# Chunk attention into a squared-ReLU FFN on one core: order of the input loads, casts behind a copy, and the first slice of w_in issued by ScalarE

## The chip, the cores and the metric

The kernel runs on one core of one Trainium2 chip. The time is the device time of one execution in microseconds (us). TensorE (PE), VectorE (DVE), ScalarE (ACT), GpSimd (POOL) and SyncE (SP) each run their own instructions in order and wait for each other by semaphores. DMAs are started by an instruction on one of these engines and are carried by 16 DMA engines.

## The reference

```python
def _attn_ref(q, k, v):                      # q, k, v: 8 x 8 x 576 x 64, float32
    # chunks of 64 tokens attend to themselves alone
    scores = scale * np.matmul(q_c, k_c.transpose(0, 1, 2, 4, 3))
    attn = np.exp(scores - np.max(scores, axis=-1, keepdims=True))
    attn = attn / (np.sum(attn, axis=-1, keepdims=True) + 1e-09)
    return np.matmul(attn, v_c)
...
x = attn_out.transpose(0, 2, 1, 3).reshape(B * S, H * D)      # 4608 x 512
h = np.maximum(x @ w_in, 0.0)                                 # w_in: 512 x 2048
return (h * h @ w_out).astype(np.float32)                     # w_out: 2048 x 512
```

## The kernel before, in words

The 4608 tokens are 18 groups of 256 tokens (four chunks of 64), and two groups are a block of 512 tokens: nine blocks, j = 0 to 8. Each block goes through the FFN in bfloat16: `ffn_in` or, from block 2 on, `ffn_in_unit` (x @ w_in, ReLU, square; the matmuls are at L607 and L494), and then `ffn_out` (L664; block 0 has its own `ffn_out_by_ft`, L781). Blocks 1 to 8 use a Strassen-like scheme with sums and differences of quarters, whose parts are named n, m, n1, n2.

Attention for later groups is put between the FFN's matmuls. The FFN of a block is a generator, and each of its steps is a slot. A table (`plan`) written by hand says after which slot a piece of attention comes, and on which slots (`go_slots`) one DMA load of a later group is issued. Pieces have short names: C casts q and k of a group to bfloat16 (CQ and CK each alone, L334 and L341; on GpSimd for groups under 8, then on ScalarE), TD transposes them by one DMA (L352, tile qkT), SC is the scores (L375) and exp (L386), AV the product with V (L403) with its division (L410, L411), XT the transpose of x (on PE, L430, with a copy at L435, for groups under 6; by DMA, L424, tile xT, from group 6 on). `nxt` is the block after the current one and `far` the one after that.

All loads and all DMA transposes are issued by SyncE, in the order in which the program says them, so that a load that stands ahead of a transpose in the program also goes ahead of it in the queue. Each DMA waits for the one eight places before it to have landed. Loads of q and k are `qk_pieces` (L106, L117, L120), those of V `v_pieces` (L148, L152): five for an even group (two of even heads, three of odd heads), four for an odd one.

The opening works on block 0 by halves of its heads: four loads of q and k (L228), eight of V (L237, into the space of `w_sum`), then the eight slices of w_in (L163), each 512 KB of float32, cast by GpSimd into `w_in_bf` (L166; the first in two halves), and the slices of w_out (L171, cast at L174). Float32 slices share five buffers named `w_st`. While PE transposes, scores and weights the first 512 tokens, `keep_busy` (L327) puts matmuls without use between. The first FFN matmul (L607) needs the first slice of w_in.

Of the kernel before, what the change touches and what calls it, by code (L numbers as in the profile page):

```python
# [17 lines left out]
def kernel(  # L18
# [9 lines left out]
    nc = tc.nc  # L28
# [128 lines left out]
        for f in pieces:  # L157
            f()

    def load_w_in(i, n_cast=1):  # L160
        cols = slice(i * 256, (i + 1) * 256)
        st = wst_pool.tile([128, 1024], FP32, name="w_st").rearrange("p (a f) -> p a f", a=n_dt)
        nc.sync.dma_start(out=st, in_=moe_w_in[:, cols].rearrange("(a p) f -> p a f", p=128))  # L163
        n = 256 // n_cast
        for c in range(0, 256, n):
            nc.gpsimd.tensor_copy(  # L166
                out=w_in_bf[:, :, i * 256 + c:i * 256 + c + n], in_=st[:, :, c:c + n])
# [77 lines left out]
    def transpose_half(src, dst, copies, by_token=False):  # L245
        flat = dst.rearrange("c t h q -> c (t h q)")
        n = 1024 // len(copies)
        if len(copies) == 1:
            banks = [bank_bf16()] * 2
            at0 = (0, 512)  # L250
        else:
            banks = [bank_bf16(), bank_bf16()]
            at0 = (0, 0)
        for h in range(2):
            cols = banks[h][:, at0[h]:at0[h] + 512].rearrange("c (n i p) -> c i n p", n=8, i=4)
            for i in range(4):
                for a in range(2):
                    nc.tensor.transpose(
                        out=cols[64 * a:64 * a + 64, i],
                        in_=src[:, 2 * h + a, i, 1::2],  # L260
                        identity=ident)
        for i, copy in enumerate(copies):
            out_, in_ = flat[:, i * n:(i + 1) * n], banks[i][:, 0:n]
            if by_token:
                out_ = out_.rearrange("c (n p i) -> c n p i", n=8, i=4)
                in_ = in_.rearrange("c (n i p) -> c n p i", n=8, i=4)
            copy(out=out_, in_=in_)
# [23 lines left out]
    def values_half(e, x, u, j):  # L291
        v_bf = v_first.bitcast(BF16)
        ps = ps_att.tile([128, 2, 512], FP32, name="ps_att")
        for t in range(2):
            for h in range(2):
                for a in range(2):
                    for p in range(2):
                        o0 = (2 * t + h) * (D + 1)
                        nc.tensor.matmul(
                            out=ps[64 * p:64 * p + 64, a, o0:o0 + D + 1],  # L300
                            lhsT=e[64 * p:64 * p + 64, a, h, 2 * j + t, :],
                            rhs=v_bf[64 * p:64 * p + 64, 2 * j + t, 4 * u + 2 * h + a, 1::2],
                            start=True, stop=True)
        o = ps[:, :, 0:4 * (D + 1)].rearrange("p a (h d) -> p a h d", d=D + 1)
        rec = att_pool.tile([128, 2, n_hp], FP32, name="rec", bufs=4)
        nc.vector.reciprocal(out=rec, in_=o[:, :, :, D])
        nc.vector.tensor_tensor(
            out=x[:, 4 * j:4 * j + 4].rearrange("p b a d -> p a b d"),
            in0=o[:, :, :, 0:D],
            in1=rec.to_broadcast([128, 2, n_hp, D]),  # L310
            op=ALU.mult)
# [494 lines left out]
    def pieces(grps):  # L806
        for g in grps:
            yield from qk_pieces(g)
        for g in grps:
            yield from v_pieces(g)  # L810
# [7 lines left out]
        kh.append(load_half(k, u, "k_sb"))  # L818
    for u in range(2):
        load_v_half(u)  # L820
    load_w_in(0, n_cast=2)
    xTs[0] = att_pool.tile([128, BT // 128, n_dt, 128], BF16, name="xT", bufs=2)
    qkTs = [att_pool.tile([128, 2, 2, n_hp, 128], BF16, name="qkT", bufs=4) for _ in range(2)]
    xs = [att_pool.tile([128, 2, n_hp, 2, D], BF16, name="x", bufs=3).rearrange(
# [8 lines left out]
    transpose_half(qh[1], qkTs[1][:, 0], [V])  # L833
    keep_busy(2)
    transpose_half(kh[1], qkTs[1][:, 1], [V, A], by_token=True)
    values_half(e0, xs[0], 0, 0)
    keep_busy(2)
    e1 = scores_half(qkTs[1])
# [34 lines left out]
    for j, grps in enumerate(blocks):  # L873
        nxt = blocks[j + 1] if j + 1 < len(blocks) else []
        far = blocks[j + 2] if j + 2 < len(blocks) else []
        plan = {}

        def at(slot, f, g):
            plan.setdefault(slot, []).append((f, g))

        if j == 0:
            loads, go_slots = pieces(far), range(17)
            at(28, sum_quarters(b11_p_b21, b11, b21), None)
            for slot, f in ((24, TA), (27, SC), (29, AV), (31, XT)):
                at(slot, f, nxt[0])
            at(31, TQ, nxt[1])
            at(31, TK, nxt[1])
            at(31, sum_quarters(b11_m_b22, b11, b22, ALU.subtract), None)
            phases = [first_ffn_in, ffn_out_by_ft(0)]
        elif j == 1:  # L890
            loads, go_slots = itertools.chain(*map(qk_pieces, far)), range(26, 48)
            for slot, f in ((4, SC), (8, AV), (12, XT)):
                at(slot, f, grps[1])
            for i, g in enumerate(nxt):
                for slot, f in ((16 + 4 * i, C), (21 + 4 * i, TD), (36 + i, SC), (38 + 2 * i, AV),
                                (41 + 2 * i, XT)):
                    at(slot, f, g)
            for i, g in enumerate(far):
                at(36 + 4 * i, C, g)
                at(42 + 3 * i, TD, g)  # L900
            at(2, sum_quarters(b11_p_b12, b11, b12), None)
            at(12, sum_quarters(b12_p_b22, b12, b22), None)
            at(20, sum_quarters(b21_p_b22, b21, b22), None)
            phases = [ffn_in(1, [(0, 256, FT_ORDER), (256, 256, FT_ORDER)]), ffn_out(1)]
        else:
            loads, go_slots = pieces(far), range(32)
            slots = {SC: (4, 4), AV: (7, 11), XT: (10, 14), C: (18, 22), TD: (20, 24)}
            if j == 3:
                slots.update({SC: (8, 8), AV: (10, 14), XT: (13, 17)})
                go_slots = [*range(6), *range(13, 17), *range(20, 32)]  # L910
            if not is_whole(nxt[0] if nxt else 0):
                slots.update({SC: (6, 8), AV: (10, 14), XT: (12, 16)})
            if j == 2:
                loads = itertools.chain(*map(v_pieces, nxt), loads)
                slots = {SC: (8, 10), AV: (12, 15), XT: (15, 18), C: (20, 23), TD: (22, 25)}
                go_slots = [*range(16), *range(25, 36)]
            late_by = 0
            if j in UNITS:
                late_by = 3
            if j == 2:  # L920
                slots.update({AV: (12, 16), XT: (15, 19)})
                go_slots = [*range(16), *range(28, 39)]
            elif j in UNITS:
                go_slots = range(35)
                if far and is_whole(far[0]):
                    go_slots = [*range(6), *range(13, 17), *range(23, 35)]
                slots.update({SC: (4, 4), AV: (8, 13), XT: (12, 17)})
                if j == 3 or not is_whole(nxt[0] if nxt else 0):
                    slots.update({SC: (8, 8), AV: (11, 16), XT: (14, 19)})
            for f in (SC, AV, XT):  # L930
                for i, g in enumerate(nxt):
                    at(slots[f][i], f, g)
            if j > 2 and far and is_whole(far[0]):
                for slot, f, i in ((16, CQ, 0), (18, CK, 0), (18, TD, 0), (18, CQ, 1),
                                   (19, CK, 1), (19, TD, 1)):
                    at(slot + late_by, f, far[i])
            else:
                for f in (C, TD):
                    for i, g in enumerate(far):
                        at(slots[f][i] + late_by, f, g)  # L940
            phases = [ffn_in_unit(j) if j in UNITS else ffn_in(j, [(0, BT, FT_ORDER)]),
                      ffn_out(j)]
        slot = 0
        for phase in phases:
            for _ in phase:
                if slot in go_slots:
                    for f in loads:
                        f()
                        break
                for f, g in plan.get(slot, []):  # L950
                    f(g)
                while late and (slot >= LATE_STORES.get(j, 99) or (j, slot) == (2, 9)):
                    late.pop(0)()
                slot += 1
        assert all(x < slot for x in plan), (j, slot, sorted(plan))
        go(loads)
        while late and j > 1:
            late.pop(0)()
# [30 lines left out]
```

## Time and profile before

| | |
|---|---|
| median of 3 runs | 280.36 us (279.69 to 280.68) |
| the profiled execution | 282.07 us, span 280.3 us |
| PE busy | 269.5 us (96%) |
| mean granted clock of TensorE | 0.993 |
| DMA queue of SyncE | 54.67 MB, 84.8% of 16 engines' span |

In the profile a line names an engine, a line of the kernel, an operation and its tiles, out<-in. Matmul records overlap, and a few can be missing. "Idle before" is time in which the engine had nothing running, with what ended it. The landing time of a DMA is when its semaphore was raised; it is read from the trace beside the issue. The clock is that which was granted to TensorE, 1.00 being full speed. Times are from the start of the span.

### The profile page before, as it was taken

To read this page: it belongs to the slowest core of one execution; us is meant where nothing else is said; L and a number is where in the kernel's file an instruction comes from. 1 tells how busy PE (TensorE), PEld (TensorE's weight loads), DVE (VectorE), ACT (ScalarE), POOL (GpSimd) and SP (SyncE) were. 2 spreads that over 40 slices of the span, in tenths; PEclk is the share of its full clock that TensorE was granted. 3 is DMA by queue.
4 is the path that set the end of the run, shared out by engine and by line. 5 is a ranking of instruction groups with operands and counts; after the bars stand their busy time and mean duration, and the time that the engine had idled before them with its cause. 6 is when DMAs were issued, how large, how long until landed. Compare 5 with 4: busy or idle time off the path is not lost.

```text
span 280.3 us, 7376 instructions
## 1 busy us (share of the span) xinstructions
PE 269.5 (96%) x3047; PEld 186.2 (66%) x3047; DVE 205.2 (73%) x313; ACT 155.7 (56%) x262; POOL 95.4 (34%) x110
## 2 busy tenths in 40 slices
PE   6987999999999999899999999999999999999995
PEld 4642445788785678457855785578558855885684
DVE  0542704899888798689868795979589949786794
ACT  1544713787426765579265927583779185507710
POOL 2036868351043810172017301720190019003403
PEclk9997999999999999999999999999999999999999
DMA  6999999989999879999999999897699992204004
GB/s 230 234 337 336 303 347 243 310 223 214 181 223 170 208 234 205 246 272 235 204 212 267 219 186 294 190 153 165 152 295 224 180 274 39 40 22 130 0 0 152
DMA packets 141313, 57.11 MB, mean 204 GB/s; under 512 B 110368, under 2 KB 135200, under 8 KB 141280
## 3 DMA queue, kind: packets, MB, share of 16 engines
q1 hardware_dynamic: 140544, 54.67, 84.8%
q0 software_dynamic: 592, 1.84, 1.7%
q8 instruction: 24, 0.39, 0.6%
q10 hardware_dynamic: 144, 0.13, 0.1%
q14 instruction: 9, 0.07, 0.1%
HBM read 36.70 MB, written 9.44 MB: 165 GB/s over the span
## 4 chain that ended last, share of the span: by engine, by line
PE 50%; DVE 0%; issue 0%
PE ps_ffn L664 24%; PE ps_ffn L607 19%; PE ps_ffn L494 6%; PE ps_att L403 1%; PE ps_att L375 1%; DVE o_sb L769 0%
## 5 line engine op out<-in xcount | busy, mean ns | idle before, releaser
L607 PE MATMUL ps_ffn<-xT,w_in_bf 128*128 128x512 bf16 (+1 forms) x528 | 112.7, 357 | 2.9 <-POOL w_in_bf L166 2.0
L620 POOL TENSOR_TENSOR gT<-rl 128x512 bf16<-128x512 f32 x40 | 45.5, 1152 | 121.5 <-ACT rl L571 118.3
L607 PEld LDWEIGHTS <-w_in_bf 128*128 128x128 bf16 x528 | 50.9, 99 | 40.8 <-POOL w_in_bf L166 2.5
L664 PEld LDWEIGHTS <-w_st 128*128 128x128 bf16 x640 | 62.2, 98 | 7.7 <-issue 0.4
L571 ACT ACTIVATE rl<-ps_ffn 128x512 f32<-128x512 f32 x84 | 50.0, 596 | 30.4 <-PE ps_ffn L607 30.2
L620 DVE TENSOR_TENSOR w_st<-gT 128x2048 bf16<-128x2048 bf16 x40 | 47.4, 1219 | 6.0 <-ACT gT L574 5.9
L664 PE MATMUL ps_ffn<-w_out_bf,w_st 128*128 128x256 bf16 x384 | 45.1, 273 | 0.0
L620 DVE TENSOR_TENSOR gT<-rl 128x512 bf16<-128x512 f32 x30 | 20.7, 691 | 21.1 <-ACT rl L571 20.7
L664 PE MATMUL ps_ffn<-w_sum,w_st 128*128 128x256 bf16 x256 | 29.6, 273 | 0.2 <-ACT n L737 0.2
L664 PEld LDWEIGHTS <-gT 128*128 128x128 bf16 x256 | 24.7, 98 | 5.0 <-ACT gT L574 0.5
L602 DVE TENSOR_TENSOR gT<-rl 128x256 bf16<-128x256 bf16 (+1 forms) x41 | 18.5, 491 | 10.2 <-ACT rl L598 9.8
L598 ACT ACTIVATE rl<-ps_ffn 128x256 bf16<-128x256 f32 (+1 forms) x48 | 20.3, 455 | 9.6 <-PE ps_ffn L607 8.9
L511 DVE SCALAR_TENSOR_TENSOR gT<-rl 128x512 bf16<-128x512 f32 x21 | 23.2, 1103 | 0.4
L411 DVE TENSOR_TENSOR x<-ps_att,rec 128x512 bf16<-128x512 f32 x32 | 22.1, 691 | 1.1
L771 ACT COPY o_sb<-ps_ffn 128x512 f32<-128x512 f32 x7 | 4.1, 585 | 30.4 <-PE ps_ffn L664 30.4
L386 ACT ACTIVATE e<-ps_att 128x1024 bf16<-128x1024 f32 x16 | 15.8, 1023 | 5.4 <-PE ps_att L375 5.4
L494 PEld LDWEIGHTS <-w_dif 128*128 128x128 bf16 x140 | 13.1, 98 | 7.5
L664 PE MATMUL ps_ffn<-w_out_bf,gT 128*128 128x256 bf16 x128 | 15.6, 273 | 0.0
L664 PE MATMUL ps_ffn<-w_sum,gT 128*128 128x256 bf16 x128 | 15.3, 273 | 0.0
L166 POOL CAST w_in_bf<-w_st 128x1024 bf16<-128x1024 f32 (+1 forms) x9 | 8.7, 969 | 19.0 <-DMA w_st<-in_moe_w_in_dram 19.0
L620 DVE TENSOR_TENSOR w_st<-xT 128x1024 bf16<-128x1024 bf16 (+1 forms) x21 | 12.5, 652 | 2.8 <-DMA xT<-x 2.0
L781 PE MATMUL ps_ffn<-w_out_bf,gT 128*128 128x512 bf16 x64 | 14.5, 380 | 0.0
(82 smaller groups left out, 294.2 us busy)
## 6 DMA issues: line engine op xcount, KB each, us to landing
q_sb<-in_q_dram SPq DMA_DIRECT2D x16, 512.0 KB, 6.4
k_sb<-in_k_dram SPq DMA_DIRECT2D x24, 256.0 KB, 6.0
out_dram<-o_sb SPq DMA_DIRECT2D x12, 512.0 KB, 4.3
w_st<-in_moe_w_in_dram SPq DMA_DIRECT2D x8, 512.0 KB, 8.6
w_st<-in_moe_w_out_dram SPq DMA_DIRECT2D x8, 512.0 KB, 6.0
ve_sb<-in_v_dram SPq DMA_DIRECT2D x28, 128.0 KB, 3.2
vo_sb<-in_v_dram SPq DMA_DIRECT2D x21, 128.0 KB, 3.1
k_sb<-in_k_dram SPq DMA_DIRECT2D x4, 512.0 KB, 6.8
```

Source lines behind the costliest of these rows:

```text
L166: nc.gpsimd.tensor_copy(out=w_in_bf[:, :, i * 256 + c:i * 256 + c + n], in_=st[:, :, c:c + n])
L386: nc.scalar.activation(out=e_out, in_=s_in, func=AF.Exp, scale=scale)
L411: nc.vector.tensor_tensor(out=x[:, t].rearrange("p h a d -> p a h d"), in0=o[:, :, :, 0:D], in1=rec.to_broadcast([128, 2, n_hp, D]), op=AL ...
L494: nc.tensor.matmul(out=out[:, 256 * f:256 * f + 256], lhsT=a[:, d, 128 * f:128 * f + 128], rhs=b[:, :, d, :], start=(first and f == 0 and ...
L511: later.append(lambda: nc.vector.scalar_tensor_tensor(out=place_of(i, jj), in0=both(x), scalar=0.0, in1=both(x), op0=ALU.max, op1=ALU.mult))
L571: nc.scalar.activation(out=rl, in_=h, func=AF.Relu)
L598: nc.scalar.activation(out=rl[:, 0:n], in_=h[:, 0:n], func=AF.Relu)
L602: nc.vector.tensor_tensor(out=gT[:, ft, c:c + n], in0=rl[:, 0:n], in1=rl[:, 0:n], op=ALU.mult)
L607: nc.tensor.matmul(out=h[:, 0:n], lhsT=w_in_bf[:, dt, ft * 128:(ft + 1) * 128], rhs=xT[:, c // 128:(c + n) // 128, dt, :], start=(dt == 0) ...
L620: engine.tensor_tensor(out=out, in0=in0, in1=in1, op=op)
L664: nc.tensor.matmul(out=outs[t], lhsT=a[:, i, t * 128:(t + 1) * 128], rhs=b[:, i, :], start=(first and i == 0 and (last or t == 0)), stop=( ...
L781: nc.tensor.matmul(out=o_ps[tt], lhsT=gT[:, ft, tt * 128:(tt + 1) * 128], rhs=w_out_bf[:, ft, :], start=(ft == 0), stop=(ft == n_ft - 1))
```

## The change

Five things are moved. No arithmetic changes, and all sizes stay.

- w_in's first slice is issued by ScalarE, behind its copy of the second half of k's transposes and ahead of the second exp, and no longer by SyncE behind V.
- In block 0 the loads are q and k of groups 4 and 5 and V of group 4. V of group 5 becomes the first loads of block 1 (slots 26 on), behind the two DMA transposes of groups 4 and 5 (slots 21 and 25).
- In block 1 XT of group 3 comes after slot 13, not 12.
- In block 2 the loads are issued on slots 0 to 11, 20 to 22 and 28 to 38, not on 0 to 15 and 28 to 38. What went out on slots 12 to 15 (q and two k of group 9, and one V) now comes behind the two XT (slots 15 and 19).
- In block 3 CQ, CK and TD of group 11 come after slots 25, 26 and 26 (with the 3 of `late_by`), not after 21, 22 and 22.

In the order of instructions on the engines, this puts: on SyncE, the transposes of groups 4 and 5 ahead of four V loads; the two xT transposes of block 3's x ahead of q, k, k and one V load; group 11's transpose behind four V loads. On ScalarE, the copy of n2 (L737) of block 3 ahead of both casts of group 11, one ReLU (L598) ahead of the copy of xT (L435) of group 3, and the DMA of w_in's first slice between a copy (L267) and an exp (L286). GpSimd's order is the same.

```diff
-    def load_w_in(i, n_cast=1):
+    def load_w_in(i, n_cast=1, queue=nc.sync):
...
-        nc.sync.dma_start(out=st, in_=moe_w_in[:, cols].rearrange("(a p) f -> p a f", p=128))
+        queue.dma_start(out=st, in_=moe_w_in[:, cols].rearrange("(a p) f -> p a f", p=128))
...
     for u in range(2):
         load_v_half(u)
-    load_w_in(0, n_cast=2)
...
     transpose_half(kh[1], qkTs[1][:, 1], [V, A], by_token=True)
+    load_w_in(0, n_cast=2, queue=nc.scalar)
     values_half(e0, xs[0], 0, 0)
...
         if j == 0:
-            loads, go_slots = pieces(far), range(17)
+            loads = itertools.chain(*map(qk_pieces, far), v_pieces(far[0]))
+            go_slots = range(17)
...
         elif j == 1:
-            loads, go_slots = itertools.chain(*map(qk_pieces, far)), range(26, 48)
-            for slot, f in ((4, SC), (8, AV), (12, XT)):
+            loads = itertools.chain(v_pieces(nxt[1]), *map(qk_pieces, far))
+            go_slots = range(26, 48)
+            for slot, f in ((4, SC), (8, AV), (13, XT)):
...
             if j == 2:
                 slots.update({AV: (12, 16), XT: (15, 19)})
-                go_slots = [*range(16), *range(28, 39)]
+                go_slots = [*range(12), *range(20, 23), *range(28, 39)]
...
             if j > 2 and far and is_whole(far[0]):
-                for slot, f, i in ((16, CQ, 0), (18, CK, 0), (18, TD, 0), (18, CQ, 1),
-                                   (19, CK, 1), (19, TD, 1)):
+                q1, k1 = (22, 23) if j == 3 else (18, 19)
+                for slot, f, i in ((16, CQ, 0), (18, CK, 0), (18, TD, 0), (q1, CQ, 1),
+                                   (k1, CK, 1), (k1, TD, 1)):
```

## The prediction

> **What bounds the kernel now.** I read the busy times first, then the slices, the waits of TensorE, the opening in order of time, and SyncE's queue around each wait.
>
> ```profile
> PE 269.5 (96%) x3047; PEld 186.2 (66%) x3047; DVE 205.2 (73%) x313; ACT 155.7 (56%) x262; POOL 95.4 (34%) x110
> PE   6987999999999999899999999999999999999995
> PEclk9997999999999999999999999999999999999999
> ```
>
> TensorE (PE) is the bound: 280.3 - 269.5 = 10.8 us without a matmul in the whole span. Only where PE waits, or where its clock drops, can an edit of order change the time. Its waits:
>
> ```profile
> PE ps_ffn L607 <- POOL w_in_bf L166: 2.0, 1, 2.0
> ...
> PE ps_ffn L607 <- DMA xT<-x: 0.9, 1, 0.9
> ...
> PE ps_att L375 <- DMA qkT<-qkb: 0.5, 1, 0.5
> PE ps_att L430 <- DVE x L411: 0.4, 1, 0.4
> ...
> PE ps_ffn L664 <- ACT n L737: 0.2, 1, 0.2
> ```
>
> Four of these stand where the change reorders: 0.9 (at 113.10), 0.5 (74.89), 0.4 (59.90), 0.2 (135.87). The fifth, 2.0 at 22.93, is the opening's. The opening in order of time (start, length, engine, line; in brackets idle time before it and what ended it), then busy times by stretch with the granted clock:
>
> ```profile
> 2.89 9.25 SPq L237 DMA_DIRECT2D w_sum<-in_v_dram  x8
> 12.19 11.08 SPq L163 DMA_DIRECT2D w_st<-in_moe_w_in_dram  x8
> 16.26 1.17 POOL L166 CAST w_in_bf<-w_st 128x512 bf16<-128x512 f32 x2 [13.98 <-DMA w_st<-in_moe_w_in_dram]
> 17.66 1.04 POOL L166 CAST w_in_bf<-w_st 128x1024 bf16<-128x1024 f32 x1 [0.24 <-DMA w_st<-in_moe_w_in_dram]
> 21.83 1.04 POOL L166 CAST w_in_bf<-w_st 128x1024 bf16<-128x1024 f32 x1 [3.12 <-DMA w_st<-in_moe_w_in_dram]
> 22.93 7.26 PE L607 MATMUL ps_ffn<-xT,w_in_bf 128*128 128x512 bf16 x25 [2.01 <-POOL w_in_bf L166]
> ```
>
> ```profile
> 20.59:24.00 3.41, 1.40 (x7) 0.51 (x6) 0.43 (x1) 1.32 (x4) 1.81 (x2) 1.00 1.08 363
> 24.00:27.41 3.41, 3.41 (x9) 1.21 (x8) 1.67 (x2) 1.36 (x3) 2.57 (x3) 0.50 0.96 321
> ```
>
> The eight slices of w_in, w0 to w7, land at 16.20, 17.61, 21.77, 23.18, 24.64 and so on: 1.3 to 1.5 apart, but 4.16 between w1 and w2. PE uses up w0 and w1 by 20.92 and waits 2.01 for w2's cast. After that stretch, 41% busy, the granted clock is 0.50 for 3.41 us, which costs half of it, 1.71. So the late w2 costs 3.7 us in this execution.
>
> **The change, part by part.** The profiled execution took 282.07 (span 280.3 and 1.8 around it); the median of the runs is 280.36, which is 1.71 less. That is the price of the clock drop, so I suppose, without proof, that most runs lack the drop. The sum is made against the profiled execution and carried over to the median.
>
> *1. V of group 5 leaves the loads of block 0 and goes behind two DMA transposes of block 1.* SyncE before:
>
> ```profile
> 64.52 1.06 SPq L148 DMA_DIRECT2D ve_sb<-in_v_dram  x2
> 65.62 1.16 SPq L152 DMA_DIRECT2D vo_sb<-in_v_dram  x2
> 66.95 5.60 SPq L352 DMA_TRANSPOSE qkT<-qkb  x2
> ```
>
> The first two rows are V of group 5 (448 KB, landing 67.39 to 68.99). The transposes land at 72.92 and 74.85, and PE's scores start 0.04 after each, the second after 0.51 of idleness. With V out of the way the first can be issued at 64.5, 2.4 earlier, and the second once Pool's k cast ends at 65.29. Both then land before their scores at 72.96 and 74.38: -0.51. V lands behind them at about 73, and values of group 5 first need it at 78.58, so it is hidden there. The queries of groups 6 and 7 follow on the same queue; they had been issued at 73.07, behind the transposes' 5.60, and should go up to 2 us sooner.
>
> *2. In block 2 the loads stop after slot 11, so that three loads of group 9 (q and two k) and one of V no longer stand ahead of the two xT transposes.* Before:
>
> ```profile
> 99.31 3.82 SPq L106 DMA_DIRECT2D q_sb<-in_q_dram  x1
> 103.17 1.78 SPq L120 DMA_DIRECT2D k_sb<-in_k_dram  x2
> 105.00 1.60 SPq L148 DMA_DIRECT2D ve_sb<-in_v_dram  x1
> 106.70 4.27 SPq L424 DMA_TRANSPOSE xT<-x  x2
> ```
>
> VectorE finishes both x by 101.4; xT lands at 112.21 and 113.05, while PE is free at 112.20. Without the 7.2 us of issuing ahead, xT lands near 106: -0.90. What is late next is group 9: its q and k land behind two xT transposes, about 1.8 later (111.2 for the last against 109.39). ScalarE casts them in order, and only its L771 copy at 112.23 stands behind, so it moves by little; the group's transposed q and k have 2.24 us of room (landing 117.73, scores at 119.97). 0.
>
> *3. In block 3 the casts of group 11 go behind the copy of n2 on ScalarE.* Before, and SyncE's transposes after them:
>
> ```profile
> 134.28 1.05 ACT L341 CAST qkb<-k_sb 128x1024 bf16<-128x1024 f32 x1 [0.64 <-DMA k_sb<-in_k_dram]
> 135.24 0.58 ACT L737 COPY n<-ps_ffn 128x512 f32<-128x512 f32 x1
> 136.91 4.60 SPq L352 DMA_TRANSPOSE qkT<-qkb  x2
> ```
>
> PE waited 0.25 for that copy: -0.25. The new cost is on SyncE: group 11's transpose now stands behind four V loads. They took 2.3 us to issue (141.56 to 143.83) and 448 KB to move, landing over 3.85 us after the transpose. Its landing was 143.59 for scores at 145.36, 1.77 of room. With PE 1.66 earlier the room is 0.11; with the transpose 2.3 later, 2.2 us would be missing, unless the queue runs ahead by the 2 us of part 1. The queue shows no pause from 88 to 146, so what it gains at 73 it should keep. Bounds 0 and +3.7 (3.85 later against 0.11 of room); I take +0.3, near the first, since 2.3 less 2 is left.
>
> *4. In block 1 the transposes of x of group 3 go one slot back.* The 0.38 at 59.90 waits for x, ready at 59.84. The ScalarE copy behind it (60.33 to 61.34) must end before PE's unit 16, at 61.42 by three units of 0.43. One slot later, the transposes end at the same time, as x is no earlier; PE does unit 13 first and then lacks it at unit 16. The relu of unit 13 (0.38) also comes ahead of the copy. Bounds -0.38 and +0.4; I take +0.05: the wait moves.
>
> *5. w0 goes to ScalarE's queue.* ScalarE's own issue of an output store lasts 0.37 and SyncE's of a w_in slice 0.37 to 0.51. It stands between the copy that ends at 11.82 and the exp at 12.34, and fits into the 0.52 idle there: 0 to +0.2. What it is moved past is V: pieces 6 to 8 land at 13.54, 14.08 and 14.61, and PE takes them at 13.76 and 15.57, so there is 0.22 and 0.96 of room. w0 is worth 1.4 us of the engines (the spacing of slices), so these can come 0 to 1.4 later and the first FFN matmul (17.30) up to 13.54 + 1.4 - 13.76 = 1.2 later. The 2.01 for w2 behind it covers that. If w2 came in time, the 1.2 would show. w0 itself gains nothing: its cast begins at 16.26 and PE is busy with attention until 17.30. w1 to w7 leave SyncE one place (0.55) sooner, but the bytes ahead of w2 are the same. Bounds for the opening: -3.7 (no wait, no drop) and +1.2; I take -0.2, near no change, as the lateness of w2 is not one of issue.
>
> The row 22.93 puts the cost in arrival, 2.01. The Trainium skill, "DMA: Bandwidth & Descriptors", section "Issuing engines are not separate DMA queues", speaks against the move: transfers share the same 16 engines whoever starts them, and a second issuer saves issue time alone. By it the opening would gain at most w_in's issue time of 0.5; no run here shows it yet.
>
> The clock row gives 0.50 after 41% busy. The skill's page "TensorE: Matmul & The Clock Gate", section "Part 1: The HAM clock gate (the "warmup" mystery)", calls the activity window free-running; by it the same idle time may or may not cost the 1.71.
>
> Sum: -0.51 - 0.90 - 0.25 + 0.3 + 0.05 - 0.2 = -1.5. Profiled: 280.6; median: 280.36 - 1.5 = 278.9.
>
> **The rivals.** *A, group 11 late (slower):* if the queue is not ahead by 145 us, TD of group 11 lands up to 3.85 later against 1.77 of room in the old time; then all earlier gains are swallowed there and the end is +2.1, 282.4. It decides from a delay of 1.77 on, and is measurably slower from 2.6. For it: the landings of those four loads; against: part 1's 2 us. *B, half of that:* the delay is about 1.8 to 2, PE waits off its gain, and the time is 280.4: no change; V late in an opening where w2 is in time (+1.2 against -1.3) gives the same, 280.3. *C, w2 comes in time:* two rings instead of one let it land near 19.0 (17.61 + 1.4); the wait goes too, in place of the -0.2 of part 5: 280.36 - 1.3 - 2.0 = 277.1. Against it: the bytes ahead of w2 are the same.
>
> **How the numbers follow.** Changes below 0.3% (0.84 us) can't be told from none. My case 0.50 (its own range 278.0 to 279.7), C 0.10, B 0.22, A 0.18. The range reaches from C's 277.0 to short of A's end, 281.2, and leaves out half of A's chance and little else. Faster: 0.47 of my case (its range passes 279.5) + 0.10 = 0.57; same: 0.22 + 0.03 = 0.25; slower 0.18.
>
> **What would show it.** Right: TensorE's waits at 74.9, 113.1 and 135.9 are gone; the first xT transpose is issued before 102; a wait for xT by ScalarE's copy near 61; the q10 queue carries w0 and V's last pieces land after 14.6. Wrong: a wait of PE for qkT near 144 over 0.5 us, the exp at 12.34 more than 0.3 later, or w2 landing before 20.

## The result, and the profile after

The changed kernel takes 283.35 us in the median of four runs (282.45 to 284.23), against 280.40 for the kernel before in four runs beside it: a ratio of 1.0109, 95% interval 1.0064 to 1.0154. It is about 3 us slower, where 1.5 us less was forecast, and lies beyond the forecast range (281.2). Run again (e9 below) it gives 1.0100 (1.0056 to 1.0145). Ratios here and below leave out executions over 1.5% above the fastest of their kernel.

The profiled execution of the changed kernel took 282.45 us (span 280.7). That is only 0.4 more than the 282.07 of the profiled execution of the kernel before, though the medians lie 3 apart; "The base of the sum" below takes this up. Its busy times, the slices, and the two queues that issue loads (packets, MB, share of 16 engines' span):

```profile
PE 270.2 (96%) x3044; PEld 187.0 (67%) x3047; DVE 203.2 (72%) x313; ACT 155.9 (56%) x262; POOL 96.0 (34%) x110
...
PE   7879999999999999999979999999999999999995
...
PEclk9979999999999999999979999999999999999999
...
q1 hardware_dynamic: 140016, 54.15, 83.7%
...
q10 hardware_dynamic: 672, 0.66, 0.8%
```

The new mark is the 7 at the twenty-first slice, in PE's row and in the clock's: something near 144 us holds PE up and then halves its clock. The queue q10 now carries w0 (0.66 MB, against 0.13 before). The view of waits of PE (us in total, times, longest) names it:

```profile
PE ps_att L375 <- DMA qkT<-qkb: 2.1, 1, 2.1
PE ps_ffn L327 <- POOL ident L72: 1.7, 1, 1.7
PE ps_att L299 <- DMA w_sum<-in_v_dram: 1.0, 3, 0.5
...
PE ps_ffn L607 <- ACT xT L435: 0.2, 1, 0.2
```

The 2.0 for w2's cast, the 0.9 for xT, the 0.5 for qkT, the 0.4 for x (L430) and the 0.2 for n2's copy are all gone. In their place stand 1.0 for V in the opening and 2.1 for a transposed q and k. The timeline of PE places the latter: group 11's 32 matmuls of scores, behind the 32 of group 10.

```profile
140.70 1.03 PE L607 MATMUL ps_ffn<-xT,w_in_bf 128*128 128x512 bf16 x4
141.66 0.45 PE L375 MATMUL ps_att<-qkT 64*64 64x64 bf16 x32
144.17 0.65 PE L375 MATMUL ps_att<-qkT 64*64 64x64 bf16 x32 [2.07 <-DMA qkT<-qkb]
```

The timeline of SyncE's queue shows what stood ahead of that transpose (start, length of the issue):

```profile
132.50 1.26 SPq L424 DMA_TRANSPOSE xT<-x  x1
133.86 1.91 SPq L352 DMA_TRANSPOSE qkT<-qkb  x1
135.82 0.58 SPq L152 DMA_DIRECT2D vo_sb<-in_v_dram  x1
136.45 1.10 SPq L148 DMA_DIRECT2D ve_sb<-in_v_dram  x2
137.59 0.51 SPq L152 DMA_DIRECT2D vo_sb<-in_v_dram  x1
138.19 2.39 SPq L352 DMA_TRANSPOSE qkT<-qkb  x1
```

Group 10's transpose goes out at 133.86, then four V loads, then group 11's at 138.19. They land at 138.81 (group 10), 139.31 to 140.89 (V) and 144.13 (group 11), and PE goes on 0.04 after that. The casts of group 11 had ended by 133.4, so ScalarE is not the cause. That the place in the queue is, e15 tests below. Busy times by stretch with the granted clock (PE, PEld, DVE, ACT, POOL, clock, DMA share, GB/s):

```profile
137.28:140.70 3.42, 3.42 (x22) 1.91 (x20) 2.18 (x5) 2.02 (x4) 0.00 (x0) 1.00 1.08 195
140.70:144.11 3.41, 1.40 (x38) 0.63 (x35) 0.97 (x2) 2.35 (x4) 1.04 (x1) 1.00 1.03 295
144.11:147.53 3.42, 3.36 (x42) 1.89 (x43) 0.69 (x1) 1.02 (x2) 0.00 (x0) 0.50 1.01 284
```

After a stretch that is 41% busy (1.40 of 3.41) the clock is 0.50 for 3.42 us, as it was in the opening of the kernel before. So in this execution the late transpose costs 2.07 and then about 1.71, half of the 3.41 (an estimate).

The account by blocks, from the first L607 matmul of each block's FFN:

| block | 0 | 1 | 2 | 3 | 4 | 5 | end |
|---|---|---|---|---|---|---|---|
| before | 17.30 | 52.46 | 84.38 | 113.10 | 141.10 | 168.56 | 280.29 |
| after | 18.37 | 51.07 | 82.42 | 110.09 | 137.67 | 168.93 | 280.67 |
| after less before | +1.07 | -1.39 | -1.96 | -3.01 | -3.43 | +0.37 | +0.38 |

Up to block 4 the change had gained 3.43 us. In block 4 it lost 3.80, which is the wait and the clock (2.07 + 1.71 = 3.78).

The opening: ScalarE issued w0 at 10.55, which took 0.43 us beside its copy of 10.54 to 11.12; it then stood idle for 0.99 until the exp at 12.12 (12.34 before), so the issue cost it nothing. V's last two pieces landed at 15.73 and 16.58 (14.08 and 14.61 before), and PE waited for them. From the timeline of the opening:

```profile
10.55 0.43 ACTq L163 DMA_DIRECT2D w_st<-in_moe_w_in_dram  x1
...
15.77 0.32 PE L299 MATMUL ps_att<-w_sum,e 64*64 64x65 bf16 x8 [0.32 <-DMA w_sum<-in_v_dram]
...
16.62 0.32 PE L299 MATMUL ps_att<-w_sum,e 64*64 64x65 bf16 x8 [0.53 <-DMA w_sum<-in_v_dram]
...
18.37 12.81 PE L607 MATMUL ps_ffn<-xT,w_in_bf 128*128 128x512 bf16 x52
...
20.53 1.04 POOL L166 CAST w_in_bf<-w_st 128x1024 bf16<-128x1024 f32 x1 [1.17 <-DMA w_st<-in_moe_w_in_dram]
```

The FFN starts 1.07 later, and w2 (landed 20.47, cast from 20.53) is in time for it. PE runs 52 matmuls without a wait, the first of them at a clock of 0.50 (17.82 to 21.23).

### The profile page after: what moved, and what is told of

It is laid out like the page before. It is cut to its first block, busy times and chain, and to the rows that moved or that the text cites. A ratio compares the mean times of both kernels' runs of the same rounds, so it can differ in the third digit from the quotient of the medians.

```text
span 280.7 us, 7374 instructions
## 1 busy us (share of the span) xinstructions
PE 270.2 (96%) x3044; PEld 187.0 (67%) x3047; DVE 203.2 (72%) x313; ACT 155.9 (56%) x262; POOL 96.0 (34%) x110
## 4 chain that ended last, share of the span: by engine, by line
PE 85%; DMA 5%; SPq 5%; DVE 3%; issue 1%; ACT 0%; DVEq 0%
PE ps_ffn L607 34%; PE ps_ffn L664 32%; PE ps_ffn L494 8%; PE ps_ffn L781 5%; SPq L237 3%; PE ps_att L403 2%; DMA qkT<-qkb 2%; DMA w_sum<-in_v_dram 2%; PE ps_att L375 2%; DMA ve_sb<-in_v_dram 2%; DVE w_st L620 1%; SPq L352 1%; PE ps_att L430 1%; SPq L228 1%; PE ps_att L191 1%
## 5 line engine op out<-in xcount | busy, mean ns | idle before, releaser
L607 PE MATMUL ps_ffn<-xT,w_in_bf 128*128 128x512 bf16 (+1 forms) x528 | 113.3, 359 | 0.2 <-ACT xT L435 0.2
L607 PEld LDWEIGHTS <-w_in_bf 128*128 128x128 bf16 x528 | 51.3, 99 | 38.0 <-issue 2.8
L598 ACT ACTIVATE rl<-ps_ffn 128x256 bf16<-128x256 f32 (+1 forms) x48 | 20.4, 454 | 8.6 <-PE ps_ffn L607 7.8
L602 DVE TENSOR_TENSOR gT<-rl 128x256 bf16<-128x256 bf16 (+1 forms) x41 | 16.9, 456 | 9.2 <-ACT rl L598 8.8
L574 ACT ACTIVATE gT<-rl 128x512 bf16<-128x512 f32 x21 | 13.2, 630 | 0.7
```

The source lines that it names most:

```text
L574: nc.scalar.activation(out=gT[:, ft], in_=rl, func=AF.Square)
L598: nc.scalar.activation(out=rl[:, 0:n], in_=h[:, 0:n], func=AF.Relu)
L602: nc.vector.tensor_tensor(out=gT[:, ft, c:c + n], in0=rl[:, 0:n], in1=rl[:, 0:n], op=ALU.mult)
L607: nc.tensor.matmul(out=h[:, 0:n], lhsT=w_in_bf[:, dt, ft * 128:(ft + 1) * 128], rhs=xT[:, c // 128:(c + n) // 128, dt, :], start=(dt == 0) ...
```

## The experiments

Two theories stood at first. *Queue place* (T in the expectations): group 11's transpose behind four V loads is the whole loss, and the other parts are gains. *Opening* (rival O): w0 on ScalarE's queue makes V late, and what was gained there in one execution is lost in most. From the first runs came two more: that part 2 (block 2) makes the last piece of group 8's V late, so that two late pieces took the gains (D), and that SyncE's queue carries too much in any order (rival F). Every ratio is to the kernel before on the same chip, with its 95% interval.

| run | kernel | ratio |
|---|---|---|
| e1 | after, part 3 undone | 1.0041 (1.0004 to 1.0077) |
| e2 | before, part 3 alone | 1.0102 (1.0054 to 1.0149) |
| e3 | after, part 5 undone | 1.0185 (1.0136 to 1.0235) |
| e4 | before, part 5 alone | 1.0011 (0.9982 to 1.0040) |
| e5 | after, both late pieces earlier | 0.9981 (0.9947 to 1.0016) |
| e6 | after, part 3 undone, V of group 8 earlier | 1.0021 (0.9988 to 1.0053) |
| e7 | before, part 1 alone | 1.0004 (0.9973 to 1.0034) |
| e8 | before, part 2 alone | 1.0031 (0.9996 to 1.0067) |
| e9 | after, again | 1.0100 (1.0056 to 1.0145) |
| e10 | e5 with fewer V loads | 0.9974 (0.9944 to 1.0003) |
| e11 | before with fewer V loads | 0.9971 (0.9939 to 1.0003) |
| e12 | e5, part 5 undone | 1.0028 (0.9994 to 1.0061) |
| e13 | e15, and V of group 8 one slot earlier | 1.0019 (0.9988 to 1.0049) |
| e14 | e13, part 5 undone | 1.0030 (1.0003 to 1.0057) |
| e15 | after, group 11's transpose first | 1.0029 (1.0005 to 1.0054) |

e1 to e4, e5 to e8, e9 to e12 and e13 to e15 each shared a chip.

**Part 3 out, and part 3 alone.** e1 takes it out of the changed kernel, e2 puts it alone into the kernel before:

```diff
-                q1, k1 = (22, 23) if j == 3 else (18, 19)
-                for slot, f, i in ((16, CQ, 0), (18, CK, 0), (18, TD, 0), (q1, CQ, 1),
-                                   (k1, CK, 1), (k1, TD, 1)):
+                for slot, f, i in ((16, CQ, 0), (18, CK, 0), (18, TD, 0), (18, CQ, 1),
+                                   (19, CK, 1), (19, TD, 1)):
```

> The changed kernel with part 3 undone (group 11's casts and transpose back at slots 21 and 22). Theory T (group 11's transpose behind four V loads makes TensorE wait 2.07 at 144 and drops the clock for 3.41, some 1.7): that wait goes, the small one for the copy of n2 (0.25) comes back, and the time falls by 2.0 + 1.7 - 0.25 = 3.5 from 283.35, to about 279.9. Rival O (the slowdown is the opening's, by w0 on ScalarE's queue): at most 1 falls away, 282.4 or more.

> The kernel before with part 3 alone. Theory T: without the head start of the other parts the transpose of group 11 lands some 2.3 to 3.9 later than 143.59, against 1.77 of room: a wait of 0.3 to 2.1 less the 0.25 of the copy, and up to 1.7 of clock where the wait is long: 280.5 to 283.9. Rival O: 280.1 to 280.4, no wait for qkT above 0.5 near 145.

Part 3 alone makes the kernel before 1.0% slower, as much as the whole change does. Without it the changed kernel is 0.4% slower: part 3 is the larger part of the loss. The 279.9 us expected of e1 did not come (281.34, and 279.52 for the kernel before beside it): undoing part 3 gave back about half of the 3.5 us that T reckoned. In e2's waits stands the same line as after:

```profile
PE ps_att L375 <- DMA qkT<-qkb: 2.2, 1, 2.2
```

In e1 it is gone (group 11's transpose lands at 142.91, its scores begin at 144.54), but another has come, which the prediction did not speak of. The timeline of PE in e1:

```profile
119.36 0.19 PE L403 MATMUL ps_att<-vo_sb,e 64*64 64x65 bf16 x1
121.58 0.19 PE L403 MATMUL ps_att<-vo_sb,e 64*64 64x65 bf16 x1 [2.04 <-DMA vo_sb<-in_v_dram]
```

That is the last piece of group 8's V. Part 2 puts it behind a 512 KB store of the output; group 9's transpose stood ahead of it before as well. It landed at 119.56 before, with its matmuls at 122.18; in e1 it landed at 121.54, with PE there at 119.5.

**w0 back on SyncE, and part 5 alone.** e3 undoes part 5 in the changed kernel, e4 makes it alone:

```diff
-    load_w_in(0, n_cast=2, queue=nc.scalar)
...
         load_v_half(u)
+    load_w_in(0, n_cast=2)
```

> The changed kernel with w0 issued by SyncE behind V again. Theory T alone: the wait at 144 stays at about 2 and the time stays within 1 of 283.35; V pieces land evenly, PE waits none for V in the opening. Rival O: the time falls by 1.5 to 3, to 280.4 to 281.9.

> The kernel before with w0 issued by ScalarE, nothing else. Theory T: the opening's delay for V (0.9 of waits in the changed kernel, first FFN matmul 1.07 later) is covered by the wait for the third slice, so 280.4 give or take 0.8. Rival O: 281.4 to 283.4, with V's last pieces at about 16.6 and the first FFN matmul at 18.4.

e4 is no different from the kernel before: the opening theory falls, and with it every gain or loss of over 0.4% by this part alone. In its profile the first FFN matmul is at 17.90 and PE waits 0.94 and 0.92 for slices of w_in. e3 is not better than the changed kernel but looks worse, beyond what either theory expected (285.35 us); its profile has both late pieces, 2.60 for V of group 8 and 2.81 for qkT.

**Both late pieces brought forward.** e5 keeps all five parts, but issues the rest of block 2's loads without the pause of slots 23 to 27, so that V of group 8 goes ahead of the transpose and the store, and in block 3 resumes the loads on slot 27, so that the transpose of group 11 goes ahead of the four V loads. e6 does the first of these and undoes part 3.

```diff
-                go_slots = [*range(12), *range(20, 23), *range(28, 39)]
+                go_slots = [*range(12), *range(20, 39)]
...
-                    go_slots = [*range(6), *range(13, 17), *range(23, 35)]
+                    go_slots = [*range(6), *range(13, 17), *range(27 if j == 3 else 23, 39 if j == 3 else 35)]
```

> The changed kernel with two repairs of SyncE's order: V of group 8 on slots 23 to 27 of block 2, ahead of group 9's transpose and of the output store, and group 11's transpose ahead of the four V loads (loads of block 3 from slot 27 on, not 23). The casts stay behind the copy of n2, and w0 stays on ScalarE. Theory D (two late pieces on a full queue took the gains: group 8's last V, a wait up to 2.6, and group 11's transpose, 2.07 to 2.8 and the clock drop of 1.7): both waits are gone, and the time is 1 to 3 below the kernel before, 276.5 to 278.5. Rival F (the queue's throughput is the floor whatever its order): a wait of 1 to 2 comes up at another piece, and the time is within 0.8 of before.

> The changed kernel without part 3 and with V of group 8 on slots 23 to 27 of block 2. Theory D: the wait of 2.04 at 121.6 that stood in the changed kernel without part 3 is gone, the wait for the copy of n2 (0.25 to 0.4) is there, and the time is 0.3 above the kernel with both repairs. Rival F: another wait of 1 to 2 and no gain on before.

Both are back at the time of the kernel before, and both of the waits are gone from their profiles. The 1 to 3 us below it that D expected did not come. In e5 three V loads now stand between the transposes of groups 8 and 9, and PE waits 1.22 for that of group 9 at 117.98; the copy of n2 is late by 0.9 in a later block. In e6 no wait of over 0.23 us is left from 20 us to the end, its profiled execution took 278.23, and yet its median is 280.82: the profiled one is the fastest of its twelve.

**Parts 1 and 2 alone.** The gains that the prediction counted, each by itself in the kernel before. The first two hunks are e7, the last is e8:

```diff
-            loads, go_slots = pieces(far), range(17)
+            loads = itertools.chain(*map(qk_pieces, far), v_pieces(far[0]))
+            go_slots = range(17)
...
-            loads, go_slots = itertools.chain(*map(qk_pieces, far)), range(26, 48)
+            loads = itertools.chain(v_pieces(nxt[1]), *map(qk_pieces, far))
+            go_slots = range(26, 48)
...
-                go_slots = [*range(16), *range(28, 39)]
+                go_slots = [*range(12), *range(20, 23), *range(28, 39)]
```

> The kernel before with part 1 alone (V of group 5 behind the transposes of groups 4 and 5). Theory D: the 0.5 at 74.9 goes, and nothing comes for it up to block 2, where the wait for xT is as before or less, since the queue is up to 2 ahead: 0.5 to 1.4 faster. Rival F: the same time as before.

> The kernel before with part 2 alone (loads of block 2 on slots 0 to 11, 20 to 22, 28 to 38). Theory D: the 0.9 for xT at 113.1 goes, and group 8's last V, now behind an output store, comes 1.5 to 3 later than 119.56 against values at 122.2 less 0.9: a wait of 0 to 1.5, and a time from 0.9 below to 1 above. Rival F: the same time, no wait for V.

Neither is measurably faster. In both profiles the wait aimed at is gone, but others have come: in e7 1.17 for xT at 110.93 and 0.75 at 134.21, in e8 this, on ScalarE and then on PE:

```profile
128.81 1.05 ACT L334 CAST qkb<-q_sb 128x1024 bf16<-128x1024 f32 x1 [0.56 <-DMA q_sb<-in_q_dram]
131.09 1.04 ACT L341 CAST qkb<-k_sb 128x1024 bf16<-128x1024 f32 x1 [1.23 <-DMA k_sb<-in_k_dram]
132.04 0.58 ACT L737 COPY n<-ps_ffn 128x512 f32<-128x512 f32 x1
```

```profile
132.67 1.58 PE L664 MATMUL ps_ffn<-w_sum,w_st 128*128 128x256 bf16 x13 [1.43 <-ACT n L737]
```

PE has come 4.4 us sooner to n2 (131.24, its start less the wait, against 135.62), but the load for ScalarE's last cast of group 11 only 3.2 sooner (that cast starts at 131.09 against 134.28). The copy that PE needs is behind it.

**The changed kernel again, and less to load.** If SyncE's queue as a whole carries too much, every gain of order must come back as a wait for some later load. To test this, e10 (from e5) and e11 (from before) leave out the loads of V of even heads from group 8 on and of odd heads from group 12 on. The values of these groups are computed from what the buffers hold, so their output is not the reference's; the work of all other engines is the same.

```diff
-        for t, p, m, b, s in runs(g):
+        for t, p, m, b, s in runs(g) if g < 8 else ():
...
-        for n, p, m, b, s in odd_loads[g]:
+        for n, p, m, b, s in odd_loads[g] if g < 12 else ():
```

> The changed kernel as it is, beside the next three on the same chip. Theory D: one or both of two waits (last V of group 8 near 120, transpose of group 11 near 145, each 1 to 2.8) and 0.7 to 1.8% slower than before. Rival F (the queue's throughput alone): the same, so this run is the yardstick, and a wait of a new kind would speak for F.

> The changed kernel with both repairs, and with the loads of V left out for even heads from group 8 on and for odd heads from group 12 on (these groups use old V, so the output is not the reference's): some 3.4 MB less on the queue, the same order otherwise. Rival F (the repaired kernel's missing gain is the queue's throughput): now the gain shows, 1.5 to 3 below the kernel before and 1 or more below the next kernel; no wait above 0.5 from 60 on. Theory D alone (no floor, the repaired order has nothing late): as the repaired kernel was, 0 to 1 below before.

> The kernel before with the same loads of V left out (output not the reference's), as the control for the one above. The waits for qkT near 75 and for xT near 113 stay, since the loads ahead of them stay: 0 to 1 below before, by F as by D. If it gains as much as the one above, the order is worth nothing even on a queue with room.

> Both repairs, and w0 issued by SyncE behind V as before. If the move of w0 brings something of its own, this is slower than the repaired kernel (0.2% below before) by 0.5 to 1; if it costs something in the opening (V late, first FFN matmul at 18.4 to 18.9 against 17.3 to 17.9), it is faster by as much; if the queue is the floor, the same within 0.4.

The changed kernel repeats its loss. Its second profile (284.44 us) shows the same wait at 144.94, of 2.95, and a clock of 0.50 for twice as long, in two stretches of the same length:

```profile
140.68:144.09 3.41, 1.31 (x37) 0.54 (x35) 0.88 (x2) 2.26 (x4) 1.04 (x1) 1.00 1.40 157
144.09:147.50 3.41, 2.56 (x39) 1.55 (x40) 0.69 (x1) 1.02 (x1) 0.00 (x0) 0.50 1.05 322
147.50:150.91 3.41, 3.41 (x22) 1.38 (x24) 0.69 (x1) 1.24 (x3) 0.00 (x0) 0.50 1.09 267
```

The wait reaches into the second stretch (2.56 of 3.41 busy). With fewer V loads both orders come to the same, 0.9974 and 0.9971. A queue too full should have let the better order show once there was room; it did not. So the fullness of the queue is not shown to be what keeps the gains of order away. Nor is it ruled out: in e11 the wait for xT near 113 is gone too, against what was expected, so there was less left for the better order to gain. e12 against e5 hints, as e3 does, that with the other parts w0 is better on ScalarE's queue, by 0.5%; the intervals overlap.

**The loss divided, and the best order.** e15 repairs only group 11's transpose. e13 also brings V of group 8 forward by one slot, ahead of the store, and so leaves group 9's transpose behind two V loads only. e14 is e13 with w0 on SyncE. The first hunk is e15, both are e13:

```diff
-                    go_slots = [*range(6), *range(13, 17), *range(23, 35)]
+                    go_slots = [*range(6), *range(13, 17), *range(27 if j == 3 else 23, 39 if j == 3 else 35)]
...
-                go_slots = [*range(12), *range(20, 23), *range(28, 39)]
+                go_slots = [*range(12), *range(20, 23), *range(27, 39)]
```

> The changed kernel with group 11's transpose ahead of the four loads of V that stood before it (block 3's loads from slot 27), and in block 2 the last piece of group 8's V one slot sooner, ahead of the output store and behind two DMA transposes no more. If the two late pieces are all that is wrong, both waits (2.07 for qkT, 0.5 to 2.6 for V) are gone and the three other edits show: 280.36 - 1.5 = 278.9, ratio about 0.995. If the other edits are worth nothing, as they were each alone, ratio 0.997 to 1.002.

> The same with the first slice of w_in issued by SyncE behind V, as before. If the place of w0 is worth nothing, the ratio is within 0.002 of the run beside it. If it is what e12 against e5 and e3 against the changed kernel hint at, it is 0.004 to 0.008 above it, and the wait for the third slice's cast (2.01 in the kernel before) stands in the profile.

> The changed kernel with group 11's transpose first and nothing else: the last piece of group 8's V stays behind a DMA transpose and the store. If the transpose of group 11 is nearly the whole loss, ratio 0.998 to 1.002. If V of group 8 costs 0.4% by itself, as the changed kernel without the late casts gave (1.0041), ratio 1.003 to 1.006 and a wait of TensorE of 0.5 to 2.6 for vo_sb near 119 to 122.

One place in the queue, group 11's transpose ahead of four V loads, takes the changed kernel from 1.0100 and 1.0109 to 1.0029: 2.0 to 2.2 us of the 3. That is less than the 3.78 read from one profile. In e15 both transposes go out in one run, at 134.81 and 137.21, and land at 139.48 and 141.28, before their scores at 141.81 and 142.09:

```profile
133.46 1.26 SPq L424 DMA_TRANSPOSE xT<-x  x1
134.81 4.69 SPq L352 DMA_TRANSPOSE qkT<-qkb  x2
139.55 0.57 SPq L152 DMA_DIRECT2D vo_sb<-in_v_dram  x1
```

The clock on record for each execution agrees. A stretch of 3.41 us at half clock takes 0.006 off the mean, so a value of 0.994 or less means at least one. All ten executions of the changed kernel (with e9), all six of e3 and five of six of e2 have it, but only four of twelve in e15 and three of twelve in e5.

The rest of 0.3% is not told apart further, and 1.0029 falls between the two ranges expected of e15. V of group 8 shows as a wait of 0.42 at 119.28 in e15 and not at all in e13, but the ratios differ by 0.1% only. In e13 other waits stand in the profile: 0.89 for xT at 137.30 and 0.81 for a transposed q and k at 200.07. w0's place makes 0.1% here (e14). Neither e13 nor e5 beats the kernel before: both are equal to it within the intervals.

## Why the prediction was wrong

**The step that failed is part 3's cost, "+0.3, near the first, since 2.3 less 2 is left".** The prediction had the place, the four loads and both bounds (0 and +3.7), and took the wrong end. All its signs of being right came, and so did one of being wrong, the wait of PE for qkT near 144. In the profile the term measured 2.07 of waiting and about 1.71 of clock in place of 0.3. Four numbers show how:

- The issue of the four loads took 2.37 us (135.82 to 138.19), as assumed (2.3). From one transpose's issue to the next it is 4.33 in the changed kernel and 2.23 before, so 2.10 more.
- The transpose then took 5.94 from issue to landing, against 4.45 before: 1.49 more. Behind the four V loads it took 5.60 to 6.12 in four profiles (changed kernel, e2, e3, e9), and 4.07 to 4.93 in the eleven with all V loads in which it follows group 10's transpose. What in flight holds it up is not shown. The whole delay is 2.10 + 1.49 = 3.59, near the 3.85 that the prediction had read from the landings of the four loads and set aside for the issue time.
- The queue was indeed ahead, and by more than the 2 assumed: group 10's transpose was issued 3.05 sooner (133.86 against 136.91).
- But PE was ahead by more still. Without the wait it would have begun the scores at 142.10 (144.17 - 2.07), which is 3.26 sooner than the 145.36 before (1.39 of it won by block 1, as the table shows). The prediction had given PE a lead of 1.66 and the queue one of 2, and had let the second cancel the delay of issue alone. Against PE the queue's head start was worth nothing. In e2, with part 3 alone, the wait is 2.2 as well.

Room of 1.77, less 3.26 for PE, plus 3.05 for the queue, less 3.59: -2.03. The wait was 2.07. So the mechanism was rival A's, a late transpose of group 11, which had a chance of 0.18; "it decides from a delay of 1.77 on, and is measurably slower from 2.6" holds, with 3.59 measured. Rival A's price was too small: it counted the wait (2.1) and not the clock behind it (1.71), though the opening of the kernel before had shown that pair.

**The other part of the miss.** The forecast was 1.5 below, the result 2.95 above, 4.45 apart; e15 puts 2.0 to 2.2 of this on the place of the transpose. Most of the rest is the gains of parts 1 to 3 (1.66 in the sum): the profiles show waits gone, the medians no gain.

**Part 1, -0.51.** The wait at 74.89 is gone. The transposes of groups 4 and 5 were issued at 62.14 and 64.24, not at 64.5 and 65.3: a larger lead than worked out. Alone it is worth nothing that can be measured (e7, 1.0004).

**Part 2, -0.90, and "What is late next is group 9 ... 0".** xT of block 3 was issued from 95.87 and landed by 102.64, and the wait at 113.10 is gone. The name of what is late next was wrong: not group 9's q and k but the last V of group 8, which the moved loads push back by one slot, behind a store, and whose 2.6 of room (119.56 to 122.18) was not counted. In the profiles it cost 0 (changed kernel) to 2.60 us (e3); alone, part 2 gives 1.0031, not a gain.

**Part 3's gain, -0.25,** came: no wait for n2 in the changed kernel. **Part 4, +0.05:** the 0.38 for x became 0.23 for ScalarE's copy, at 60.01; the wait moved, as forecast, and is 0.15 shorter, where 0.05 more was forecast.

**Part 5, -0.2.** The bounds held, and its side effects came as described: V's last pieces landed 1.65 and 1.97 later, a little beyond the 1.4 allowed, and the first FFN matmul 1.07 later (up to 1.2 forecast). In the profile of the changed kernel w2 was in time, which is rival C's case, but without its landing near 19.0 (rival C's end is 277.1 by its own sum, not the 277.0 that the range has): it came at 20.47, and the price was the late start and a clock of 0.50 for 3.41 us from 17.82. Alone the part measured 1.0011 (e4). The Trainium skill, "DMA: Bandwidth & Descriptors", section "Issuing engines are not separate DMA queues", holds that a second issuing engine saves issue time alone, since the transfers share the 16 engines; e4 agrees, and V's later landing fits the sharing.

**The base of the sum.** The profiled execution before (282.07) was not a typical one. In the five batches the kernel before has medians of 278.99 to 280.40, and of the seven other profiles with w0 on SyncE's queue e2 alone shows such a wait for a cast of w_in (2.4); in e3, e7, e8, e11, e12 and e14 no such wait is over 0.52. Most runs lack the drop, as supposed: of 116 executions of the kernel before in the four later batches 26 have a clock of 0.994 or less, and 90 one of 0.998 or more. But that the drop is the price of 1.71 is not borne out: set against the median of its batch, the middle one of the 26 is no longer than the middle one of the 90 (within 0.1 us). Of the profiles most lack the wait for w2 too, and so part of what looks gained in the changed kernel's profile (1.39 at block 1) may not have been there to be gained in the median. The two profiled executions lie 0.4 us apart and the medians 3, since the one before was 1.67 above its median and the one after 0.90 below its own.

**What stays open.** Why the gains of parts 1 and 2, plain in the profiles as waits that are gone, are not in the medians. In e7 and e8 other waits had come in their place, which suffices for these two profiles; but e6 has none of over 0.23 from 20 us on, with 278.23 us in its profiled execution, and a median of 280.82. Executions of one kernel lie up to 4.1 us apart (e8: 278.90 to 282.99), and one profile of each can't say which waits the others had. A full queue as the common reason was tested (e10, e11) and neither confirmed nor ruled out. The place of w0 with the other parts in is open too: better on ScalarE's queue by 0.5% in e12 against e5, by 0.8% in e3 against the changed kernel and by 0.1% in e14 against e13, each within overlapping intervals.

## What to carry to other kernels

When a load is moved in a queue that is always busy, list every transfer that thereby comes behind another, and set its room against the distance between landings, not against the time that the issues take: here 2.4 us of issuing became 3.6 us of lateness. A lead of the queue counts only against the lead of the engine that consumes, and a change that makes TensorE earlier takes its own cover away. Where a wait of 2 us on TensorE is possible, price the clock behind it as well. Read several executions before pricing a wait from one: the opening's wait of 2.0 for w2, which stood in the profile before, was at most 0.52 in six of seven others with the same order of opening.

## What the runs showed of the hardware

*A wait of the same length may or may not cost the clock.* In e3 a wait of 2.60 us for V ended at 121.34 and the clock stayed at 1.00; one of 2.81 ended at 146.74 and was followed by 0.50. Cut into stretches of 3.41 us, counted back from the drop at 147.03:

```profile
116.31:119.72 3.41, 2.43 (x68) 1.52 (x56) 2.50 (x3) 2.61 (x4) 2.99 (x3) 1.00 1.00 283
119.72:123.13 3.41, 1.79 (x23) 1.11 (x23) 2.84 (x6) 0.49 (x1) 0.67 (x1) 1.00 0.82 207
143.61:147.02 3.41, 0.60 (x64) 0.49 (x60) 0.69 (x1) 1.49 (x2) 0.45 (x1) 1.00 0.75 203
147.03:150.44 3.41, 3.41 (x32) 1.82 (x20) 0.69 (x1) 1.54 (x2) 0.00 (x0) 0.50 0.99 310
```

The first wait is split over two stretches, which are still 71% and 52% busy; the second falls into one, 18% busy. In e1 a wait of 2.04 also left the clock at 1.00. This fits what the Trainium skill says on the page "TensorE: Matmul & The Clock Gate", section "Part 1: The HAM clock gate (the "warmup" mystery)", that the window over which activity is counted runs freely. Then it matters where in it a wait falls. The traces bear out the free running as far as the changes of the clock go: in every profile with more than one drop they lie a whole number of 3.413 us apart (changed kernel: 17.82, 144.11 and 280.65, which is 37 and 40 of them). But the busy share alone draws no line here. In the changed kernel's opening a stretch 60% busy (14.41 to 17.82, 2.06 of 3.41) was followed by 0.50, and in e3 one 52% busy was not.

*A second issuing queue takes from the first.* One 512 KB load on ScalarE's queue, started while SyncE's V loads were under way, moved the landing of V's last two pieces by 1.65 and 1.97 us against the profile before, where slices of that size land 1.3 to 1.5 us apart on one queue. Executions differ here too. V's last piece landed at 14.47 to 15.88 in the eight profiles with w0 on SyncE's queue, and at 16.18 to 18.41 in the eight in which ScalarE issued w0 ahead of that piece. In e9, where that piece was issued at 10.76 and w0 at 11.52, it landed at 15.32.
